# Block-sparse attention and a cosine MLP: the half-exchanging copies of the transposed queries go from SyncE's queue to GpSimd's, with a new order of steps

## The chip, the cores and the metric

The kernel runs on one core of a Trainium2 chip. The metric is the device time of one execution in microseconds (us). The kernel before was timed three times: 850.83, 857.53 and 858.05 us, with a median of 857.53 us. One further execution was profiled; every duration below that is read from a view of the trace belongs to that execution.

## The reference, cut to what matters

```python
# attention: q, k, v are 4 x 8 x 768 x 64 (batch, heads, positions, head size)
scores = matmul(q, k.T) / sqrt(64)
# blocks of 32 positions. A query block sees its neighbours, the first and the last block,
# and 3 sampled blocks; the first and the last query block see everything
scores = where(mask, scores, -1e9)
attn   = exp(scores - max(scores)) ;  attn = attn / sum(attn)
a      = matmul(attn, v)                       # fp32
x      = a in rows of (batch, position)        # 3072 x 512
h      = x @ w_in                              # w_in 512 x 2048
out    = (h * cos(h)) @ w_out                  # w_out 2048 x 512, fp32 result
```

## The kernel before, in words

**Tiles.** The queries are worked in 24 tiles of 128 positions, six for each of the four batches: five sparse tiles and one dense tile (the first and the last blocks, which see all keys). A tile has eight heads. The kernel keeps fp32 quality with fp16 matmuls: every operand is split into a high and a low fp16 part, and products are taken of several pairs of parts.

**The transposed queries.** Before a tile can be multiplied with the keys, its queries must lie with the head dimension on partitions. `prep_q` makes this in a tile U of 128 partitions. `U[:, 0]` holds the transposed queries with the high parts on partitions 0 to 63 and the low parts on 64 to 127; `U[:, 1]` holds the same with the two halves exchanged. For tiles 0 to 3 TensorE makes both. For the 20 tiles from 4 to 23 a transposing DMA (`u_transpose`, L1447, step name uT) writes `U[:, 0]`, and two plain DMAs of 64 x 1024 elements (`u_swap`, L1454 and L1452, step name uc) copy the halves crosswise into `U[:, 1]`. They wait for the transposing DMA. U has two slots, so the U of a tile can be filled while the tile before it is in use. In the trace's rows they are one name, U; in the rows of program order they are U_93 and U_94.

**A tile's attention.** A sparse tile is four units of two heads, a dense tile eight units of one head. For each unit: TensorE scores (L1520, L1521, L1526; L1537 dense) read U; VectorE takes the maximum (L1553); ScalarE the exponential (L1575) and the high part (L1585); VectorE the low part (L1589) into one of three `ring` buffers; SyncE issues a transposing DMA from the ring to one of three PT tiles (L1604); TensorE multiplies PT with V (L1614, L1626; L1640 dense). V comes partly through plain DMAs from SyncE (L1483, L1486), partly through indirect DMAs that GpSimd issues, four for each sparse tile (`v_gather`, L1492). V has two slots.

**The MLP.** At the end of a tile VectorE and ScalarE scale and split its rows (L1662, L1664, L1666), and SyncE issues a transposing DMA to half of a tile xT (L1669). With both halves there, TensorE does the up-projection of the 256 rows (L1801); ScalarE evicts (L1810) and takes the cosine (L1828); VectorE reduces the argument and multiplies (L1820, L1824, L1833, L1842), ScalarE makes the high part (L1839); TensorE does the down-projection (L1851), ScalarE evicts it (L1870), and SyncE stores it (L1875). The exponential and the cosine belong to different function tables of ScalarE, so a switch between them costs a table load.

**The order.** Nothing is ordered at run time except by semaphores. `plan_kernel` makes a list of steps, each with an engine, a cost, a position `pos` and its operands; `Plan.run` takes them one by one, the ready step with the smallest position first, and the program is issued in that order on each engine. A step's position is its due place plus the corrections of a table, `NUDGES`, looked up by the step's name: for `uc` of tile 23, `uc`, `uc23`. So both an edit of a step's engine and the table's numbers set the order. SyncE's queue executes its DMA issues strictly one after the other, and one that waits holds those behind it; the same holds of GpSimd's.

Of the kernel before, what the change touches and what calls it, by code (L numbers as in the profile page):

```python
# [81 lines left out]
    wc25_0=1.55, wc25_1=0.25, wc25_2=-1.23, wsq25=4.27, wl26=11.94, wc26=-8.12, wc26_0=-16.55, wc26_1=-1.96, wc26_2=-11.56, wsq26=7.92, wl27=0.35,
    wc27=-3.37, wc27_0=-5.24, wc27_1=5.68, wc27_2=49.47, wsq27=4.91, wred24=-15.24, wsc24=-0.49, whi24=-4.49, wlo24=-9.29, whi25=1.62, wlo25=19.32,
    whi26=33.15, wlo26=-4.66, wl28=-8.97, wc28=5.55, wc28_0=-0.52, wc28_1=0.13, wsq28=-6.28, wl29=-1.2, wc29=-61.45, wc29_0=5.2, wc29_1=7.84,
    wc29_2=-31.01, wsq29=-38.92, wl30=8.34, wc30=-9.45, wc30_0=12.37, wc30_1=31.8, wc30_2=20.24, wsq30=0.34, wl31=14.98, wc31=-0.21, wc31_0=-6.47,
    wc31_1=5, wc31_2=-2.32, wsq31=26.29, wred28=4.21, wsc28=5.26, whi28=-19.62, wlo28=-6.21, whi30=2, wlo30=0.25, wmax=15.33, ql1=-5.72, qsq1=-14.68,
    qsc1=3.98, qnu1=1.34, qhi1=-47.08, qlo1=-6.38, uT1=-18.81, up1=-3.53, vg1=-17.37, vg1_0=-9.27, vg1_2=0.1, vi1=30.91, vi1_0=0.48, vi1_1=-18.54,
    vi1_2=0.12, vi1_3=0.12, qk=-0.17, qk0=-58.98, qk0_0=0.24, mx=0.27, mx0=-2.49, mx0_0=-21.81, nb=-3.59, nb0=-8.96, nb0_0=2.59, ex=1.35, ex0=-3.07,
    ex0_0=-22.48, ph=-3.63, ph0=-21.88, ph0_0=-4.4, pl=-21.9, pl0=-22.66, pl0_0=-3.74, PT=-0.26, PT0=4.89, PT0_0=-4.28, pv=0.3, pv0_0=-5.56,
    qk0_1=0.86, mx0_1=-11.94, nb0_1=2.39, ex0_1=2.98, ph0_1=-5.55, pl0_1=15.27, PT0_1=-2.63, pv0_1=6.05, qk0_2=7, mx0_2=-13.62, nb0_2=7.03,  # L90
    ph0_2=0.14, pl0_2=-16.04, PT0_2=-3.48, pv0_2=15.14, qk0_3=18.43, mx0_3=-9.04, nb0_3=9.8, ex0_3=-3.71, ph0_3=7.63, pl0_3=-9.05, PT0_3=-7.28,
    pv0_3=-3, rs=-2.94, rs0=-31.95, rr=-6.44, rr0=6.78, no=0.17, no0=-18.12, xh=0.87, xh0=12.96, xl=0.07, xl0=-4.32, xT=-3.02, xT0=12.24, xp=-14.84,
    xp0=4.93, wgd1=-25.62, wga1=-4.93, ql2=3.86, qsq2=0.31, qsc2=-12.49, qu2=10.26, qnu2=7, qhi2=-4.29, qlo2=-24.12, uT2=-4.61, up2=0.35, vg2=-4.52,
# [429 lines left out]
def plan_kernel(env, B, H, S, D, DM, DFF, pr):  # L523

    pl = Plan()
    e = env
# [166 lines left out]
    def prep_q(n, pos):  # L693
# [25 lines left out]
        for k in range(0 if by_pe else 2):  # L719
            op("SP", 0, pos, lambda k=k: e.u_swap(U.t, k), r=[(U, 0)], w=[(U, 1 + k)], dma=0.364, hw=0.625, name=f"uc{n}")  # L720
# [1209 lines left out]
```

## Time and profile before

| what | before |
|---|---|
| median of three runs | 857.53 us (850.83, 857.53, 858.05) |
| profiled execution, own time | 853.78 us |
| its span in the trace | 851.5 us, so 2.3 us lie around it |
| mean granted TensorE clock | 0.936 |
| busy: TensorE, VectorE, ScalarE, GpSimd | 85%, 76%, 73%, 12% |
| plain half-exchanging copies | 40, of 128 KB each, all issued from SyncE |
| indirect gathers | 80, all issued from GpSimd |

PE in the rows is TensorE, DVE VectorE, ACT ScalarE, POOL GpSimd and SP SyncE. "SPq" is SyncE's queue in the act of issuing a DMA, and the duration there is that of the issue, not of the transfer. A busy share is a mean over stages: the first 200 us fetch and split the keys, values and weights of the start, the middle alternates attention with the MLP, and the last 70 us or so are the MLP alone.

### The profile page before, as it was taken

What the parts mean: (1) busy time and instruction counts of PE and PEld (TensorE: products, weight loads), DVE (VectorE), ACT (ScalarE), POOL (GpSimd) and SP (SyncE); (2) the same over time, 40 slices, a digit from 0 to 9 for tenths busy, and PEclk for the clock granted to TensorE, in tenths of its full rate; (3) what the DMA queues carried; (4) which work ended last, traced back from release to release, by engine and by line L of the source; (5) the groups of instructions that cost most, each with busy time, mean ns of one, the idle gap of its engine ahead of it and who ended that gap; (6) DMA issues with size and microseconds to landing.
All of it is one profiled execution on the core that took longest, in us unless ns stands there. A gap on an engine that the chain in (4) does not pass through costs nothing.

```text
span 851.5 us, 23033 instructions
## 1 busy us (share of the span) xinstructions
PE 727.7 (85%) x9272; PEld 506.8 (60%) x9272; DVE 644.8 (76%) x1632; ACT 624.8 (73%) x1193; POOL 101.8 (12%) x128
## 2 busy tenths in 40 slices
PE   3556667779999869987999979999988869999997
PEld 2444554546767537656767548677665548576583
DVE  3999989998967776878668876879578746867352
ACT  1686846888867898788758978779669857769342
POOL 5211231000030101200020111000020111000000
PEclk9965697879999979999999999999999989999999
DMA  9999893398895989899979999989696997855300
GB/s 253 324 208 275 211 264 98 73 233 166 213 222 127 201 164 194 157 230 149 228 159 182 196 177 170 216 133 165 191 156 116 184 196 155 181 83 118 87 2 25
DMA packets 313306, 146.54 MB, mean 172 GB/s; under 512 B 266224, under 2 KB 290928, under 8 KB 313200
## 3 DMA queue, kind: packets, MB, share of 16 engines
q1 hardware_dynamic: 308080, 129.35, 73.1%
q0 software_dynamic: 5120, 15.73, 8.4%
q8 instruction: 72, 1.18, 0.6%
q14 instruction: 34, 0.28, 0.1%
HBM read 68.23 MB, written 12.58 MB: 95 GB/s over the span
## 4 chain that ended last, share of the span: by engine, by line
PE 40%; ACT 12%; DMA 11%; DVE 10%; issue 3%; SPq 1%; DVEq 0%; ACTq 0%
PE ph L1801 19%; PE po L1851 15%; DMA PT<-ring 6%; ACT P L1575 4%; DVE P L1553 3%; DMA W<-kn 2%; DMA xT<-n 2%; ACT ring L1585 2%; DVE ring L1589 1%; PE xp L1640 1%; PE xp L1626 1%; PE sp L1520 1%; DVE hs L1833 1%; DVE g L1842 1%; DVE g L1824 1%
## 5 line engine op out<-in xcount | busy, mean ns | idle before, releaser
L1801 PE MATMUL ph<-xT,w 128*128 128x256 f16 x2304 | 270.8, 278 | 10.1 <-DMA xT<-n 6.7
L1851 PE MATMUL po<-w,g 128*128 128x512 f16 x1152 | 269.0, 383 | 8.6 <-ACT g L1839 7.1
L1801 PEld LDWEIGHTS <-w 128*128 128x128 f16 x2304 | 226.5, 99 | 47.6 <-issue 7.3
L1851 PEld LDWEIGHTS <-g 128*128 128x128 f16 x1152 | 108.2, 98 | 128.0 <-ACT g L1839 7.4
L1575 ACT ACTIVATE P<-P,sm 128x352 f32<-128x352 f32 (+1 forms) x224 | 151.9, 679 | 28.8 <-DVE sm L1570 19.3
L1492 POOL DMA_INDIRECT V<-scr,gidx x80 | 89.2, 1115 | 613.4 <-PE xp L1614 316.0
L1589 DVE TENSOR_TENSOR ring<-P,ring 128x704 f16<-128x704 f32 (+1 forms) x112 | 100.1, 906 | 31.5 <-ACT ring L1585 30.1
L1810 ACT ACTIVATE hs<-ph,sm 128x512 f32<-128x512 f32 x96 | 64.4, 680 | 50.8 <-PE ph L1801 42.8
L1585 ACT CAST ring<-P 128x704 f16<-128x704 f32 (+1 forms) x112 | 86.5, 785 | 13.0 <-DMA PT<-ring 11.9
L1553 DVE CUSTOM_DVE_ANT_1 P<-sp,bias 128x352 f32<-128x352 f32 x160 | 77.7, 518 | 14.1 <-PE sp L1526 13.1
L1833 DVE SCALAR_TENSOR_TENSOR hs<-hs,sm,g 128x1024 f32<-128x1024 f32 x48 | 61.0, 1281 | 23.6 <-ACT g L1828 22.4
L1520 PE MATMUL sp<-W,U 128*128 128x192 f16 x320 | 53.2, 268 | 29.2 <-DVE sm L1553 27.7
L1828 ACT ACTIVATE g<-g,sm 128x1024 f32<-128x1024 f32 x48 | 54.7, 1146 | 23.7 <-DVE g L1824 23.4
L1842 DVE TENSOR_TENSOR g<-hs,g 128x1024 f16<-128x1024 f32 x48 | 58.6, 1223 | 17.1 <-ACT g L1839 16.9
L1839 ACT ACTIVATE g<-hs 128x1024 f16<-128x1024 f32 x48 | 50.4, 1051 | 18.2 <-DVE hs L1833 17.5
L1824 DVE SCALAR_TENSOR_TENSOR g<-g,hs 128x1024 f32<-128x1024 f32 x48 | 58.3, 1220 | 0.5
L1521 PEld LDWEIGHTS <-U 128*128 128x128 f16 x320 | 33.4, 104 | 35.7 <-issue 32.0
L1614 PE MATMUL xp<-V,PT 96*32 96x64 f16 x1920 | 31.0, 202 | 22.0 <-DMA PT<-ring 18.8
L1820 DVE TENSOR_SCALAR g<-hs 128x1024 f32<-128x1024 f32 x48 | 32.9, 691 | 21.8 <-ACT hs L1810 20.1
L1521 PE MATMUL sp<-W,U 128*128 128x64 f16 x320 | 48.7, 207 | 0.0
L1626 PE MATMUL xp<-V,PT 128*128 128x64 f16 x960 | 45.5, 201 | 0.0
L1614 PEld LDWEIGHTS <-PT 96*32 96x32 f16 x1920 | 21.6, 102 | 37.7 <-DMA PT<-ring 25.9
(176 smaller groups left out, 896.0 us busy)
## 6 DMA issues: line engine op xcount, KB each, us to landing
V<-scr SPq DMA_DIRECT2D x20, 384.0 KB
stage<-in_k_dram SPq DMA_DIRECT2D x12, 512.0 KB
w<-in_moe_w_in_dram SPq DMA_DIRECT2D x12, 512.0 KB
w<-in_moe_w_out_dram SPq DMA_DIRECT2D x12, 512.0 KB
V<-scr SPq DMA_DIRECT2D x8, 768.0 KB
scr<-n SPq DMA_DIRECT2D x21, 256.0 KB
qs<-in_q_dram SPq DMA_DIRECT2D x20, 256.0 KB
U<-U SPq DMA_DIRECT2D x40, 128.0 KB
```

The lines of the kernel that those rows point to most:

```text
L1492: self.nc.gpsimd.indirect_dma_start(V[:96, 2 + j, :], None, self.scr[b][:, :], bass.IndirectOffsetOnAxis(ap=self.gidx[:96, c : c + 1], axi ...
L1521: mm(spv[:, :, 96:128].rearrange("p y (n c) -> p y n c", c=hf), u, ends, start=False, stop=False)
L1553: self.nc.vector.tensor_tensor_reduce(out=self.p_view(n, Pt)[:, a].rearrange("p (n c) -> p n c", c=hf), in0=sp[:, :w].rearrange("p (n c) - ...
L1575: self.nc.scalar.activation(Pv[:, a], Pv[:, a], AF.Exp, scale=qc[:, 4:5], bias=nb[:, bcol : bcol + 1], accum_out=sums[:, 2 * j + a : 2 * j ...
L1585: self.nc.scalar.copy(R[:, :, 0, : self.width(n)], self.p_view(n, Pt))
L1589: self.nc.vector.tensor_tensor(R[:, :, 1, :w], self.p_view(n, Pt), R[:, :, 0, :w], ALU.subtract)
L1801: self.nc.tensor.matmul(ph[:, ff, :], self.W1[p][:, wl, cc, c * P : (c + 1) * P], xT[:, xl * NCC + cc, :], start=(j == 0), stop=(j == len( ...
L1810: self.nc.scalar.activation(hs[:, h * 512 : h * 512 + 512], ph.rearrange("p f t -> p (f t)"), AF.Copy, scale=self.turns[b][:, p : p + 1])
L1824: self.nc.vector.scalar_tensor_tensor(kt, kt, MAGIC, hs, op0=ALU.subtract, op1=ALU.subtract)
L1833: self.nc.vector.scalar_tensor_tensor(hs, hs, c[:, p : p + 1], kt, op0=ALU.mult, op1=ALU.mult)
L1842: self.nc.vector.tensor_tensor(g[:, 1024:2048], hs, g[:, 0:1024], ALU.subtract)
L1851: self.nc.tensor.matmul(po, g[:, gl, ff, t * P : (t + 1) * P], self.W2[p][:, wl, ff, :], start=(first and ff == half * hf and j == 0), sto ...
```

## The change

The two copies of `u_swap` are issued by GpSimd and not by SyncE, the planner's entry for the step says so, and the whole table NUDGES has new numbers (2731 entries before, 2720 now; nearly every one differs). The other parameters of the planner are as they were. The file is a line shorter ahead of the functions, so all lines are one lower: L1454 is now L1453, L1452 is L1451, L1492 is L1491.

```diff
@@ prep_q
         for k in range(0 if by_pe else 2):
-            op("SP", 0, pos, lambda k=k: e.u_swap(U.t, k), r=[(U, 0)], w=[(U, 1 + k)], dma=0.364, hw=0.625, name=f"uc{n}")
+            op("POOL", 0.85, pos, lambda k=k: e.u_swap(U.t, k), r=[(U, 0)], w=[(U, 1 + k)], dma=0.364, name=f"uc{n}")
@@ u_swap
         if k:
-            self.nc.sync.dma_start(U[D : 2 * D, 1], U[0:D, 0])
+            self.nc.gpsimd.dma_start(U[D : 2 * D, 1], U[0:D, 0])
         else:
-            self.nc.sync.dma_start(U[0:D, 1], U[D : 2 * D, 0])
+            self.nc.gpsimd.dma_start(U[0:D, 1], U[D : 2 * D, 0])
@@ NUDGES
...
```

**SyncE, batch 3, where the MLP's xT of tiles 18 and 19 is transposed.** Before, the second of the two DMAs into xT stands behind the two copies of the U of tile 22, in the slot U_93:

```order
L1447 DMA_TRANSPOSE U_93<-n_91 128x8x128
L1669 DMA_TRANSPOSE xT_108<-n_90 128x8x128
L1604 DMA_TRANSPOSE PT_104<-ring_99 128x12x128
L1454 DMA U_93<-U_93 64x1024
L1452 DMA U_93<-U_93 64x1024
L1669 DMA_TRANSPOSE xT_108<-n_89 128x8x128
L1483 DMA V_106<-scr_122 96x2048
```

The same place on SyncE in the changed kernel, from the transpose of the same U on:

```order
L1446 DMA_TRANSPOSE U_93<-n_90 128x8x128
L1603 DMA_TRANSPOSE PT_102<-ring_99 128x12x128
L1485 DMA V_106<-scr_122 16x2048
L1668 DMA_TRANSPOSE xT_109<-n_89 128x8x128
L1603 DMA_TRANSPOSE PT_104<-ring_101 128x12x128
L1603 DMA_TRANSPOSE PT_103<-ring_100 128x12x128
L1603 DMA_TRANSPOSE PT_102<-ring_99 128x12x128
L1668 DMA_TRANSPOSE xT_109<-n_91 128x8x128
```

The copies are gone from the queue; the second xT now stands behind three PT transposes and no copies, where one PT and two copies stood ahead of it.

**GpSimd, batches 1 to 3.** Before, nothing but gathers stands there (V_105 and V_106 are the two slots of V, scr_120 to scr_122 the values of batches 1 to 3, "x4" four in a row):

```order
L1492 DMA V_105<-scr_120,gidx 96x1024 x4
L1492 DMA V_105<-scr_121,gidx 96x1024 x4
L1492 DMA V_106<-scr_121,gidx 96x1024 x8
L1492 DMA V_105<-scr_121,gidx 96x1024 x8
L1492 DMA V_105<-scr_122,gidx 96x1024 x4
L1492 DMA V_106<-scr_122,gidx 96x1024 x4
```

In the changed kernel, from the gathers of batch 3's first tile on (tiles 18 and 19, then the copies of tiles 20, 21 and 22 in among the gathers of tile 20):

```order
L1491 DMA V_105<-scr_122,gidx 96x1024 x4
L1491 DMA V_106<-scr_122,gidx 96x1024 x4
L1453 DMA U_93<-U_93 64x1024
L1451 DMA U_93<-U_93 64x1024
L1491 DMA V_106<-scr_122,gidx 96x1024 x3
L1453 DMA U_94<-U_94 64x1024
L1451 DMA U_94<-U_94 64x1024
L1491 DMA V_106<-scr_122,gidx 96x1024
L1453 DMA U_93<-U_93 64x1024
L1451 DMA U_93<-U_93 64x1024
```

Every pair of copies now follows gathers and precedes others; the last gather of tile 20 stands behind the pair of tile 21.

**ScalarE, in the middle of the program.** Before, cosines (L1828) are taken in pairs between two table loads:

```order
L1828 ACTIVATE g_83<-g_83,sm 128x1024
L1828 ACTIVATE g_85<-g_85,sm 128x1024
L1839 ACTIVATE g_83<-hs_81 128x1024
L1839 ACTIVATE g_85<-hs_82 128x1024
L1810 ACTIVATE hs_81<-ph_116,sm 128x512
L1575 ACT_TABLE_LOAD
L1575 ACTIVATE P_97,sm<-P_97,sm 128x352
```

In the changed kernel there is a place at which one cosine is taken alone between exponentials (L1574):

```order
L1574 ACT_TABLE_LOAD
L1574 ACTIVATE P_96,sm<-P_96,sm 128x352
L1663 CAST n_89<-ot_111 128x512
L1574 ACTIVATE P_96,sm<-P_96,sm 128x352
L1574 ACTIVATE P_95,sm<-P_95,sm 128x352
L1584 CAST ring_99<-P_96 128x2x352
L1574 ACTIVATE P_95,sm<-P_95,sm 128x352
L1827 ACT_TABLE_LOAD
L1827 ACTIVATE g_84<-g_84,sm 128x1024
L1584 CAST ring_100<-P_95 128x2x352
L1574 ACT_TABLE_LOAD
```

Over the whole program ScalarE has 40 table loads where it had 36. Apart from these and from the 40 copies, the number of instructions on each engine is what it was.

More of the change, by code (lines that the diff above doesn't have):

```diff
@@ new lines @@
+    wc23_1=-3.68, wc23_2=-18.82, wsq23=-25.39, wred20=-25.2, wall20=9.18, wsc20=13.17, whi20=-11.29, wlo20=0.51, whi22=-1.17, wlo22=13.45,
+    wl24=-3.52, wc24=7.36, wc24_0=-7.67, wc24_2=5.08, wsq24=13.27, wc25=-0.99, wc25_0=3.07, wc25_1=10.39, wc25_2=3.33, wsq25=13.34, wl26=2.29,
+    wc26=-7.06, wc26_0=-19.8, wc26_1=-5.48, wc26_2=-32.37, wsq26=15.59, wl27=-2.08, wc27_0=-13.87, wc27_1=-4.5, wc27_2=37.1, wsq27=14.79,
+    wred24=-15.66, wall24=-0.06, wsc24=2.66, whi24=-10.93, whi25=3.87, wlo25=18.54, whi26=21.69, wlo26=-2.06, wl28=-7.57, wc28=6.22, wc28_0=-2.17,
@@ new lines @@
+    pl8_0=1.74, PT8=5.36, PT8_0=0.84, pv8=6.93, pv8_0=-3.37, qk8_1=-1.48, mx8_1=0.91, nb8_1=-2.39, ex8_1=15.48, ph8_1=-5.46, pl8_1=-13.82,
+    PT8_1=-1.94, pv8_1=-1.39, qk8_2=-4.22, mx8_2=-3.02, nb8_2=-0.23, ex8_2=-8.54, ph8_2=5.41, pl8_2=-3.01, PT8_2=-0.59, pv8_2=-5.8, qk8_3=-2.01,
+    mx8_3=-5.71, nb8_3=-4.06, ex8_3=-0.73, ph8_3=-4.82, pl8_3=0.39, PT8_3=-5.3, pv8_3=0.89, rs8=-0.76, rr8=19.38, no8=21.01, xh8=9.46, xl8=-7.94,
+    xT8=-1.62, vload2=-27.97, vload2_0=10.85, vsq2=11.13, vsq2_0=-20.33, vsq2_1=-41.91, vload2_1=-20.36, vsq2_2=-8.03, vsq2_3=-31.17,
@@ new lines @@
+    pv11=3.25, pv11_0=37.99, qk11_1=-0.64, mx11_1=-0.91, nb11_1=-7.22, ex11_1=-24.51, ph11_1=-6.45, pl11_1=-10.61, PT11_1=-7.48, pv11_1=7.93,
+    qk11_2=-0.49, mx11_2=-1.61, nb11_2=-0.24, ex11_2=-1.27, ph11_2=-1.28, pl11_2=-14.18, PT11_2=-2.09, pv11_2=-7.29, qk11_3=-0.21, mx11_3=-0.99,
+    nb11_3=-3.52, ex11_3=20.4, ph11_3=-0.15, pl11_3=1.61, PT11_3=0.62, pv11_3=-41.33, qk11_4=0.2, mx11_4=0.09, nb11_4=6.17, ex11_4=-99.02,
+    ph11_4=-2.88, pl11_4=9.49, PT11_4=2.28, pv11_4=-16.63, qk11_5=1.89, mx11_5=1.34, nb11_5=1.91, ex11_5=-13.29, ph11_5=-3.31, pl11_5=-7.73,
@@ new lines @@
+    ksq3_0=-3.14, ksq3_1=9.8, kload3_1=-6.64, ksq3_2=10.5, ksq3_3=9.59, kload3_2=14.89, ksq3_4=23.64, ksq3_5=-20.56, kred3=5.13, kall3=7.11,
+    ksc3=-8.81, wgd16=3.96, wga16=-4.68, m7=5, m7_0=4.15, ev7=1.46, ev7_0=7.14, ka7=-3.93, ka7_0=3.47, kb7=0.92, kb7_0=-16.9, sin7=-11.16,
+    sin7_0=-2.81, gm7=21.81, gm7_0=1.66, gh7=-4.81, gl7=16.41, gl7_0=7.58, ev7_1=11.92, ka7_1=-1.31, kb7_1=8.83, sin7_1=1.34, gm7_1=30.63,
+    gh7_1=-14.38, gl7_1=20.95, m7_2=1.06, ev7_2=7.24, ka7_2=-4.75, kb7_2=1.3, sin7_2=34.59, gm7_2=2.74, gh7_2=23.69, gl7_2=-16.41, m7_3=0.51,
@@ new lines @@
+    ev7_3=-0.4, ka7_3=-3.69, kb7_3=-8.32, sin7_3=-46.78, gm7_3=-5.36, gh7_3=22.84, gl7_3=-19.38, d7=6.17, d7_0=0.2, d7_1=1.53, d7_2=-32.22,
+    d7_3=2.22, o7=0.63, o7_0=-11.11, st7=17.23, st7_0=-1.07, o7_1=2.93, st7_1=-16.13, ql17=-4.14, qsq17=-1.61, qsc17=-21.94, qnu17=18.75,
+    qhi17=-9.63, qlo17=7.74, uT17=9.45, uc17=-27.88, vg17=15.95, vg17_0=10, vg17_1=0.26, qk16=1.19, qk16_0=-13.54, mx16=16.1, mx16_0=-0.87,
+    nb16=-1.51, nb16_0=-8.87, ex16=-1.1, ex16_0=-12.33, ph16=4.32, ph16_0=-7.87, pl16=-4.8, pl16_0=-17.53, PT16=1.64, PT16_0=1.9, pv16_0=1.58,
@@ new lines @@
+    qk16_1=-9.23, nb16_1=-2.51, ex16_1=8.54, ph16_1=-5.17, PT16_1=4.86, pv16_1=-23.36, qk16_2=0.08, mx16_2=-1.04, nb16_2=-14.79, ex16_2=-6.31,
+    pl16_2=15.04, PT16_2=2.97, pv16_2=20.34, qk16_3=-0.23, mx16_3=-4.14, nb16_3=-13.46, ex16_3=-53.73, ph16_3=-5.6, pl16_3=-1.05, PT16_3=12.71,
+    pv16_3=2.08, rs16=9.29, rr16=-5.91, no16=-4.92, xh16=-2.28, xl16=12.81, xT16=6.76, qk17_0=-0.86, mx17=11.66, mx17_0=-2.91, nb17=-0.42,
+    nb17_0=-6.12, ex17=4.48, ex17_0=14.18, ph17=-0.35, ph17_0=-2.94, pl17=-6.91, pl17_0=-11.84, PT17=6.82, PT17_0=-7.79, pv17=0.6, pv17_0=1.5,
@@ new lines @@
+    pl20_0=2.23, PT20=-4.38, PT20_0=2.21, pv20_0=0.04, qk20_1=-5.86, mx20_1=-6.12, nb20_1=5.23, ex20_1=2.48, ph20_1=-4.19, pl20_1=38.52,
+    PT20_1=-0.63, pv20_1=-7.03, qk20_2=-4.42, mx20_2=-0.83, nb20_2=6.13, ex20_2=-17.94, ph20_2=0.56, pl20_2=27.45, pv20_2=0.26, qk20_3=-6.31,
+    mx20_3=-4.82, nb20_3=2.55, ex20_3=3.51, ph20_3=1.62, pl20_3=0.11, PT20_3=17, pv20_3=-9.44, rs20=6.1, rr20=-8.88, no20=16.42, xh20=11.12,
+    xl20=-12.76, xT20=-3.62, wgd21=15.17, wga21=-7, ql22=29.17, qsq22=-0.62, qsc22=-16.47, qu22=-4.78, qnu22=4.81, qhi22=2.74, qlo22=6.2, uT22=1.62,
@@ new lines @@
+    uc22=3.41, vg22=-5.99, vg22_1=14.91, vg22_2=35.17, vi22=1.12, vi22_0=4.4, vi22_1=-29.51, vi22_2=39.46, vi22_3=-1.55, qk21=-1.23, qk21_0=2.67,
+    mx21=-5.35, mx21_0=-2.72, nb21=1.89, nb21_0=-0.23, ex21=2.23, ex21_0=1.15, ph21=4.78, ph21_0=-13.6, pl21=-30.31, pl21_0=0.79, PT21_0=-0.73,
+    pv21=3.67, pv21_0=-2.65, qk21_1=6.62, mx21_1=1.03, nb21_1=-7.01, ex21_1=-5.79, ph21_1=-22.52, pl21_1=-3.14, PT21_1=-1.22, pv21_1=-6.68,
+    qk21_2=4.48, mx21_2=-0.98, nb21_2=-3.56, ex21_2=28.45, ph21_2=-12.55, pl21_2=8.57, PT21_2=3.7, pv21_2=-3.39, qk21_3=2.32, mx21_3=3.56,
@@ L304 @@
+    sin11_1=24.62, gm11_1=-3.01, gh11_1=17.86, gl11_1=69.07, m11_2=3.68, ev11_2=-0.47, ka11_2=28.68, kb11_2=-10.83, sin11_2=10.83, gm11_2=-8.23,
+    gh11_2=-8.3, gl11_2=-0.96, m11_3=0.01, ev11_3=2.87, ka11_3=-0.66, kb11_3=-14.95, sin11_3=-14.65, gm11_3=5.5, gh11_3=-21.88, gl11_3=-53.81,
+    d11=19.18, d11_0=1, d11_2=71.36, d11_3=-19.97, o11=3.47, o11_0=-6.52, st11=17.36, st11_0=29.43, o11_1=-3.25, st11_1=55.16,
 )
```

456 lines of the change are left out of this document (210 added, 246 removed).

## The prediction

> **What bounds the kernel now.** I read the page first: the span, the busy shares and the chain that ended last.
>
> ```profile
> span 851.5 us, 23033 instructions
> PE 727.7 (85%) x9272; PEld 506.8 (60%) x9272; DVE 644.8 (76%) x1632; ACT 624.8 (73%) x1193; POOL 101.8 (12%) x128
> PE 40%; ACT 12%; DMA 11%; DVE 10%; issue 3%; SPq 1%; DVEq 0%; ACTq 0%
> PE ph L1801 19%; PE po L1851 15%; DMA PT<-ring 6%; ACT P L1575 4%; DVE P L1553 3%; DMA W<-kn 2%; DMA xT<-n 2%; ACT ring L1585 2%; DVE ring L1589 1%; PE xp L1640 1%; PE xp L1626 1%; PE sp L1520 1%; DVE hs L1833 1%; DVE g L1842 1%; DVE g L1824 1%
> ```
>
> TensorE works 85% of the span, and 40% of the chain is its own. SyncE's queue, from which the copies are taken, is 1% of the chain, some 8.5 us for everything it issues. Next I cut the span into stages and looked where TensorE idles.
>
> ```profile
> core 0: us, PE busy (x) PEld busy (x) DVE busy (x) ACT busy (x) POOL busy (x), PEclk, DMA share, GB/s
> 0.00:200.00 200.00, 127.54 (x1827) 92.44 (x1828) 175.09 (x466) 134.67 (x258) 41.10 (x68) 0.80 0.85 214
> 200.00:650.00 450.00, 417.40 (x5206) 291.55 (x5205) 347.12 (x881) 362.06 (x706) 49.15 (x48) 0.98 0.90 179
> 650.00:700.00 50.00, 37.00 (x717) 22.84 (x717) 35.98 (x133) 38.52 (x94) 7.35 (x8) 0.91 1.02 176
> 700.00:851.00 151.00, 145.71 (x1525) 99.97 (x1523) 86.65 (x154) 89.54 (x136) 4.21 (x4) 0.99 0.47 95
> ```
>
> The first column after the stretch is its length, the second TensorE's busy time. TensorE idles 72.5 us in the first 200, 32.6 in the next 450, 13.0 in the 50 after that and 5.3 at the end. So 51 us of idle time lie in the stretches where 18 of the 20 pairs of copies are issued; that is all that a freer queue could win there. The waits say which of it hangs on SyncE's transposes.
>
> ```profile
> PE xp L1614 <- DMA PT<-ring: 18.8, 18, 3.4
> PE ph L1801 <- DMA xT<-n: 6.7, 5, 3.2
> ```
>
> TensorE waited 18.8 us for PT in 18 places and 6.7 us for xT in five. Nobody is listed as waiting for a copy of U itself.
>
> **What is removed: 40 issues on SyncE.**
>
> ```profile
> L1447 SPq DMA_TRANSPOSE U<-n x20: 1231/1402/3248, 113.0 to 727.2; - x20
> L1454 SPq DMA_DIRECT2D U<-U x20: 472/538/1137, 117.7 to 734.5; - x20
> L1452 SPq DMA_DIRECT2D U<-U x20: 587/594/1402, 118.3 to 735.4; - x20
> ```
>
> By the medians a pair holds the queue 0.538 + 0.594 = 1.13 us, twenty pairs 22.6 us. What counts is where a PT or an xT that is waited for stands behind a pair. In the chain this happens in one place:
>
> ```profile
> 379.12 0.74 SPq L1604
> 379.98 0.79 SPq L1454
> 380.82 0.60 SPq L1452
> 381.85 5.01 DMA PT<-ring
> ```
>
> Here 0.79 + 0.60 = 1.4 us go. The second place is the xT of tiles 18 and 19, where the order of SyncE changes as shown above. The first four rows are SyncE's and VectorE's timelines, the last TensorE's:
>
> ```profile
> 688.11 1.14 SPq L1454 DMA_DIRECT2D U<-U  x1
> 689.29 0.60 SPq L1452 DMA_DIRECT2D U<-U  x1
> 689.98 2.59 SPq L1669 DMA_TRANSPOSE xT<-n  x1
> 688.49 0.74 DVE L1666 TENSOR_TENSOR n<-ot,n 128x512 f16<-128x512 f32 x1
> 698.20 4.05 PE L1801 MATMUL ph<-xT,w 128*128 128x256 f16 x20 [3.20 <-DMA xT<-n]
> ```
>
> The data were ready at 688.49 + 0.74 = 689.23, the issue came at 689.98, and TensorE then waited 3.20 us: 0.75 us are the copies'. In the new order three PT transposes stand ahead of the second xT in their place, so this 0.75 may be lost again. I count it as won, and the doubt goes into the order below. Sum: **-2.1 us**. The other pairs that stand directly ahead of a PT aren't on the chain; of six such places this is the last:
>
> ```profile
> 587.34 0.59 SPq L1452 DMA_DIRECT2D U<-U  x1
> 588.03 1.71 SPq L1604 DMA_TRANSPOSE PT<-ring  x1
> ```
>
> If all six counted at 1.13 us, another 6.8 us would go: the far end of this term is -8.9 us. Its near end is 0, where something else is late by as much.
>
> **What is added: 40 issues on GpSimd.** The trace shows no plain copy from GpSimd. The nearest rows are the gathers, from the page, from the view of their line and from GpSimd's timeline:
>
> ```profile
> L1492 POOL DMA_INDIRECT V<-scr,gidx x80 | 89.2, 1115 | 613.4 <-PE xp L1614 316.0
> L1492 POOL DMA_INDIRECT V<-scr,gidx x80: 914/921/5593, 35.5 to 720.3; - x80
> DMA to landing us min/median/max: 3.1/5.8/11.5
> 498.45 0.92 POOL L1492 DMA_INDIRECT V<-scr,gidx  x1 [0.30 <-issue]
> ```
>
> With 0.92 + 0.30 = 1.22 us each, 40 copies take 49 us of GpSimd, which is busy 102 of 851 us and idle 613 ahead of the gathers, 316 of it because a slot of V isn't free. That is the cover. It would be gone where a gather stands behind a copy that waits for its transpose of U; but the transposes of tiles 20 to 22 stand well ahead of those gathers' use, and TensorE isn't listed as waiting for a gather. I take 0 for GpSimd's own time.
>
> The second price is the landing. On SyncE the first copy of a pair holds the second back by 0.54 us at the median and by 1.14 at most (0.84 in the middle), on GpSimd by 1.22 us, some 0.4 more. Two tiles have the least room, 9 (the first two rows) and 23 (the rest):
>
> ```profile
> 306.70 0.60 SPq L1452 DMA_DIRECT2D U<-U  x1
> 312.85 0.25 PE L1520 MATMUL sp<-W,U 128*128 128x192 f16 x1
> 727.25 1.23 SPq L1447 DMA_TRANSPOSE U<-n  x1
> 730.67 3.69 SPq L1604 DMA_TRANSPOSE PT<-ring  x2
> 735.35 0.60 SPq L1452 DMA_DIRECT2D U<-U  x1
> 741.17 0.81 PE L1537 MATMUL sp<-W,U 128*128 128x384 f16 x4
> ```
>
> From the second copy's start to the first matmul that reads U there are 312.85 - 306.70 = 6.15 us in tile 9 and 5.82 in tile 23. With the 0.4 us taken off, 5.75 and 5.4 are left; the median gather lands in 5.8. Tile 23 has more in truth: its copies stood behind two PT issues (730.67, 3.69 us) that GpSimd doesn't have ahead of them. So with a landing of 5.8 us tile 9 is late by 0.1 and tile 23 not at all; I take **+0.3 us**. With the quickest gather (3.1 us) it is 0, with the slowest (11.5) in both tiles 5.8 + 6.1 = 12 us.
>
> The longest gather took 5.59 us to issue where the median took 0.92, and the mean 1115 ns stands 0.19 us over the median. The Trainium skill, "SBUF — State Buffer", section "SBUF: two separate sides", speaks against the change: a DMA issued from GpSimd needs its descriptors written by GpSimd's cores, these are locked out while VectorE runs a two-port operation, and a DMA from SyncE or ScalarE isn't. The trace agrees in that some gathers are stretched, but doesn't show by what. By that rule the sum would carry 40 x 0.19 = 7.8 us more of GpSimd (an estimate from the row), of which two late tiles would see 0.4 us; without it nothing.
>
> **What is moved: the order.** ScalarE gets four more table loads:
>
> ```profile
> L1575 ACT ACT_TABLE_LOAD  x17: 1283/1283/1283, 158.8 to 779.1; - x17
> L1828 ACT ACT_TABLE_LOAD  x18: 1283/1283/1283, 119.3 to 786.8; - x18
> L1828 ACT ACTIVATE g<-g,sm x48: 1132/1148/1154, 124.0 to 830.7; 128x1024 f32<-128x1024 f32 x48
> 300.17 1.28 ACT L1828
> 652.73 1.28 ACT L1575
> ```
>
> The last two are the first and the last of five that stand on the chain; 5 of 35 loads. Four more are 4 x 1.283 = 5.1 us of ScalarE, and 5/35 of that **+0.7 us** of the path (bounds 0 and 5.1). The rest of the order reads much the same: the number of PT issues ahead of each xT on SyncE differs by a few at most, and the last stage has the same work. Whether the new order fits the chip's durations better or worse can't be read from before's trace. Its bounds are what I can name: the 51 us of idle time after 200 us from one side, and the same from the other; of these the 25.5 us that TensorE waits for PT and xT are the part that SyncE's order sets directly. I take **0**, nearest to the rows that don't change, and keep a third of 25.5, some 8 us, to both sides.
>
> **The sum** against the profiled execution's own 853.8 us (851.5 and 2.3 around it): 853.8 - 2.1 + 0.3 + 0.7 = 852.7, rounded to **852**. The median before, 857.5, is 4 us higher than that execution, so against the median 852 would read as 0.6% faster. About 1% is what a measurement of this kernel can tell from no change: its three runs lie 7.2 us apart.
>
> **The rivals.**
>
> *SyncE was the hidden limit of the attention stages.* For it: the six pairs that stand directly ahead of a PT, and the stretch from 650 to 700 us, where TensorE is busy only 37 of 50 us. Against it: the queue is 1% of the chain. Then the whole -8.9 us is won and the new order, made for the freer queue, adds what is left of one third of the PT and xT waits, 2 us more: 853.8 - 8.9 - 2 + 0.7, near **843 us**. The Trainium skill, "DMA: Bandwidth & Descriptors", section "Issuing engines are not separate DMA queues", limits this rival: it says that another issuing engine saves only the sequencer's time, so the transfers themselves (5.01 us of PT in the chain above) would be no shorter. By that rule nothing beyond the 22.6 us of issue can come from the move itself. No run here shows it yet.
>
> *The exchanged half comes late.* The slower side: copies from GpSimd that land like the slower gathers. It decides from a landing of some 5.4 us, in tiles 9 and 23. With 10 us there tile 9 is late by 4.3 and tile 23, if it isn't pulled forward, by 4.6; 853.8 - 2.1 + 0.7 + 4.3 + 4.6 is **861 us**, and with 11.5 us 864. For it: gathers do reach 11.5 us, and GpSimd's issue stretches to 5.59. Against it: a pair of the U of most tiles is issued long ahead of its use, since U has two slots.
>
> *The copies' move does nothing, and the new order alone decides, for the worse*: a cosine alone between exponentials holds the next exponential by two loads and the cosine's 1.148 us, 3.7 us in all, and four more loads are two such places, 7.4 us; with the 0.75 of the xT lost too and nothing won it is 853.8 + 8.2 = **862 us**.
>
> **How the numbers follow.** My forecast, 852, within 1% of the runs before: 0.44. SyncE as the limit, 843: 0.33, nearly all of it faster by over 1%. Exchanged half late, 861: 0.10. The order for the worse, 862: 0.13. Of the two slow cases most lies over 1% slower than the profiled execution. So faster 0.34, same 0.44, slower 0.22. The forecast alone, with the bounds of order and tables, reaches from 845 to 860; with the faster rival down to 838 and the two slower ones up to 866 some 2 in 10 are left out.
>
>
> **What would show it.** In the trace after: no U on SyncE, 40 issues of about 0.9 us on GpSimd at 0.3 us distance (right if the sum of GpSimd's busy time rises by some 40 us). The wait of TensorE for PT falls by 1 to 3 us and not by 9, or the first rival is true. Waits of TensorE's score matmuls for a DMA of U appear in tiles 9 and 23 at most, and are under 1 us; a row of several us there is the second rival. 40 table loads, of which about six on the chain. The forecast is wrong if the idle time of TensorE in the stretch from 200 to 700 us changes by more than 8 us without the copies showing it: then the order was the change.

## The result, and the profile after

The changed kernel is slower. Beside the runs of the kernel before on the same chip (median of all of them 857.06 us) it takes 883.82 us in the median; the ratio is 1.030 (95% interval 1.021 to 1.039). The forecast was 852 us with a range of 838 to 866. The profiled execution took 883.01 us. One thing is needed to read the ratios below: in some of the comparisons everything on the chip, the kernel before too, took 893 to 899 us where it took 855 to 858 us in the others, so each ratio stands with the time of before beside it.

The page after, as before: span, busy time, the chain by engine and by line.

```profile
span 881.2 us, 23095 instructions
PE 739.1 (84%) x9272; PEld 511.2 (58%) x9272; DVE 644.2 (73%) x1632; ACT 630.0 (71%) x1197; POOL 125.0 (14%) x168
PE 43%; DMA 24%; DVE 19%; ACT 7%; issue 5%; DVEq 1%; SPq 1%; ACTq 0%
PE ph L1800 18%; PE po L1850 16%; DMA PT<-ring 13%; DMA xT<-n 5%; DVE P L1552 3%; DVE ring L1588 2%; DMA W<-kn 2%; PE sp L1519 2%; PE xp L1625 2%; ACT P L1574 1%; PE sp L1525 1%; DVE hs L1832 1%; PE xp L1639 1%; DVE g L1823 1%; PE sp L1536 1%
```

VectorE's busy time is what it was, and ScalarE's is 5.2 us longer, of which the four table loads are 5.1. The transposes into PT have gone from 6% of the chain to 13%, those into xT from 2% to 5%. For the stages I cut both executions where TensorE has done the same 60% and 85% of its work (worked out by counting the matmuls of each line). The first three rows are before, the last three after. The second stage begins within tile 16 (its first scores stand at 510 us before and 527 after) and ends shortly ahead of the scores of tile 23 (741 and 771 us); it is called the late stage below.

```profile
0.00:535.00 535.00, 435.03 (x5834) 308.94 (x5835) 434.43 (x1149) 407.35 (x805) 82.75 (x108) 0.91 0.90 196
535.00:730.00 195.00, 176.91 (x2305) 121.63 (x2302) 142.63 (x364) 149.15 (x284) 19.07 (x20) 0.97 0.90 166
730.00:851.00 121.00, 115.71 (x1162) 76.21 (x1145) 67.78 (x121) 68.29 (x106) 0.00 (x0) 1.00 0.37 78
...
0.00:548.00 548.00, 437.48 (x5816) 308.44 (x5820) 431.35 (x1143) 410.30 (x803) 91.98 (x132) 0.88 0.87 188
548.00:759.00 211.00, 185.53 (x2308) 126.31 (x2308) 147.52 (x375) 153.10 (x291) 31.94 (x34) 0.92 0.80 159
759.00:881.00 122.00, 116.11 (x1162) 76.43 (x1160) 65.33 (x116) 66.58 (x104) 1.10 (x2) 1.00 0.40 80
```

Of the 30 us between the two spans 13 lie in the first stage, 16 in the second, which is not half as long, and 1 in the third. The 13 can't simply be put down to the change: a second profile of the kernel before, shown below, took 546 us for the same stage. In the second stage TensorE idles 25.5 us instead of 18.1, and the same matmuls take 185.5 us instead of 176.9; the granted clock is 0.92 there instead of 0.97 (185.5 x 0.92 and 176.9 x 0.97 are nearly the same).

What TensorE waits for after:

```profile
PE xp L1613 <- DMA PT<-ring: 27.7, 20, 4.2
PE xp L1639 <- DMA PT<-ring: 7.2, 4, 4.0
PE ph L1800 <- DMA xT<-n: 9.0, 6, 2.6
```

All three have risen (18.8, 2.4 and 6.7 us before; 22.2, 1.2 and 5.9 in the second profile of before); a wait for a copy of U isn't among them. The copies on GpSimd themselves are cheap:

```profile
L1453 POOL DMA_DIRECT2D U<-U x20: 516/551/607, 119.6 to 763.8; - x20
U<-U POOLq DMA_DIRECT2D x40, 128.0 KB, 4.3
```

An issue takes 0.55 us (the other half's line, L1451, has 0.56), and the data land 4.3 us later in the median. Nothing waits for them.

### The profile page after: what moved, and what is told of

It reads as the page before. It is cut to its first block, busy times and chain, and to the rows that moved or that the text cites. A ratio compares the mean times of both kernels' runs of the same rounds, so it can differ in the third digit from the quotient of the medians.

```text
span 881.2 us, 23095 instructions
## 1 busy us (share of the span) xinstructions
PE 739.1 (84%) x9272; PEld 511.2 (58%) x9272; DVE 644.2 (73%) x1632; ACT 630.0 (71%) x1197; POOL 125.0 (14%) x168
## 4 chain that ended last, share of the span: by engine, by line
PE 43%; DMA 24%; DVE 19%; ACT 7%; issue 5%; DVEq 1%; SPq 1%; ACTq 0%
PE ph L1800 18%; PE po L1850 16%; DMA PT<-ring 13%; DMA xT<-n 5%; DVE P L1552 3%; DVE ring L1588 2%; DMA W<-kn 2%; PE sp L1519 2%; PE xp L1625 2%; ACT P L1574 1%; PE sp L1525 1%; DVE hs L1832 1%; PE xp L1639 1%; DVE g L1823 1%; PE sp L1536 1%
## 5 line engine op out<-in xcount | busy, mean ns | idle before, releaser
L1850 PE MATMUL po<-w,g 128*128 128x512 f16 x1152 | 271.8, 385 | 2.4 <-DVE g L1841 1.1
L1574 ACT ACTIVATE P<-P,sm 128x352 f32<-128x352 f32 (+1 forms) x224 | 151.9, 680 | 52.5 <-DVE sm L1569 34.7
L1491 POOL DMA_INDIRECT V<-scr,gidx x80 | 91.2, 1140 | 267.8 <-PE xp L1613 152.2
L1588 DVE TENSOR_TENSOR ring<-P,ring 128x704 f16<-128x704 f32 (+1 forms) x112 | 99.3, 905 | 27.7 <-ACT ring L1584 27.6
L1827 ACT ACTIVATE g<-g,sm 128x1024 f32<-128x1024 f32 x48 | 54.7, 1146 | 18.1 <-DVE g L1823 17.9
L1453 POOL DMA_DIRECT2D U<-U x20 | 10.8, 542 | 365.6 <-DMA U<-n 262.8
L1613 PE MATMUL xp<-V,PT 96*32 96x64 f16 x1920 | 31.6, 202 | 33.4 <-DMA PT<-ring 27.7
L1520 PEld LDWEIGHTS <-U 128*128 128x128 f16 x320 | 33.8, 105 | 31.4 <-issue 27.7
```

The source lines that it names most:

```text
L1491: self.nc.gpsimd.indirect_dma_start(V[:96, 2 + j, :], None, self.scr[b][:, :], bass.IndirectOffsetOnAxis(ap=self.gidx[:96, c : c + 1], axi ...
L1520: mm(spv[:, :, 96:128].rearrange("p y (n c) -> p y n c", c=hf), u, ends, start=False, stop=False)
L1574: self.nc.scalar.activation(Pv[:, a], Pv[:, a], AF.Exp, scale=qc[:, 4:5], bias=nb[:, bcol : bcol + 1], accum_out=sums[:, 2 * j + a : 2 * j ...
L1588: self.nc.vector.tensor_tensor(R[:, :, 1, :w], self.p_view(n, Pt), R[:, :, 0, :w], ALU.subtract)
L1850: self.nc.tensor.matmul(po, g[:, gl, ff, t * P : (t + 1) * P], self.W2[p][:, wl, ff, :], start=(first and ff == half * hf and j == 0), sto ...
```

## The experiments

**Which half of the change costs?** In two kernels the order is held fixed on every engine, and only the queue of the copies is exchanged: the old order with the copies on GpSimd, and the new order with the copies on SyncE. The planner's entry stays, so that no step moves.

```diff
 e1 (in the kernel before)
-            self.nc.sync.dma_start(U[D : 2 * D, 1], U[0:D, 0])
+            self.nc.gpsimd.dma_start(U[D : 2 * D, 1], U[0:D, 0])
 e2 (in the changed kernel)
-            self.nc.gpsimd.dma_start(U[D : 2 * D, 1], U[0:D, 0])
+            self.nc.sync.dma_start(U[D : 2 * D, 1], U[0:D, 0])
 ... and the other half alike
```

> The order of before is kept step for step on every engine; only the 40 copies are issued from GpSimd, each at its old place in the program. If the new order is what costs (my theory now), this takes 853 to 859 us, like before. If the queue costs (copies that land late or gathers held behind them), it takes about 880 us. If both have a part, 865 to 872.

> The order of the changed kernel is kept step for step; only the 40 copies are issued from SyncE, each at its place in the program. If the new order costs, this takes 880 us or more (SyncE now has the copies too, up to 27 us of issue). If GpSimd's queue costs, it falls back to about 857 us.

Measured, with before at 899.2 us: 891.43 us, 0.989 (0.983 to 0.994), for the copies alone, and 901.38 us, 1.003 (0.999 to 1.007), for the order alone. Neither is the 3% of the first comparison, so the changed kernel was run again beside both.

> The changed kernel again, now beside its two halves. The halves (copies alone 0.989, order alone 1.003, on a chip where before takes 899 us) multiply to 0.992. If the parts add up, this is 0.99 to 1.00 of before, and the 3% belongs to the chip of the first comparison. If copies and order hurt only together, it is 1.03 of before as in the first comparison.

> The kernel before with a profile on this chip: about 899 us if the chip is the one of the first four experiments, 857 if it is that of the first comparison; its PT, xT and score waits are what the others are compared with.

> Copies alone, as in the first experiment: 0.985 to 0.995 of before if that gain is the kernel's and not the chip's; 1.00 to 1.01 if it is the chip's.

> Order alone, as in the second experiment: 1.00 of before if the chip doesn't matter; 1.03 where the changed kernel takes 1.03, if the order is what costs there.

| order, queue of the copies | ratio, before at 855.57 us | ratio, before at 899.2 us |
|---|---|---|
| old order, GpSimd | 1.002 (0.998 to 1.006) | 0.989 (0.983 to 0.994) |
| new order, SyncE | 1.012 (1.004 to 1.021) | 1.003 (0.999 to 1.007) |
| new order, GpSimd (the change) | 1.027 (1.019 to 1.035) | 1.006 and 1.002, below |

The profiled execution of before took 862.25 us here. Where before takes 856 us, moving the copies costs nothing while the old order stays, and the new order costs 1.2% by itself. Both together cost 1.5% more than the new order alone (1.027 over 1.012). The intervals overlap a little, and the two profiled executions lie only 3 us apart (867.54 and 870.41 us), so that the copies hurt in the new order and not in the old is likely but not shown. Where before takes 899 us, the copies alone gain 1.1%, and the changed kernel loses little against before; against the old order with the copies on GpSimd the new order costs 1.4% there too (1.003 over 0.989).

**Is it the numbers of the table or the planning with GpSimd?**

```diff
 e3 (the kernel before, with its table, and with both edits of code)
+            op("POOL", 0.85, pos, ..., dma=0.364, name=f"uc{n}")
 e4 (the changed kernel, with its table, and both edits of code undone)
+            op("SP", 0, pos, ..., dma=0.364, hw=0.625, name=f"uc{n}")
```

> The old table of corrections, but the planner is told that the copies are GpSimd's, so it works out its order anew from the old numbers; the copies are issued from GpSimd. If it is the new numbers that cost, this stays within 1.5% of before (850 to 870 us). If any order that the planner makes with the copies on GpSimd is bad, it is near 880 us.

> The new table of corrections, with the copies told to the planner as SyncE's and issued there. If the new numbers cost by themselves, this is 875 to 895 us. If they cost only together with GpSimd's queue, it is near 857 us.

Measured, with before at 899.2 us: 931.96 us, 1.034 (1.029 to 1.039), and 928.41 us, 1.033 (1.028 to 1.038). Each table costs over 3% when the planner reckons the copies on the other queue. What I expected of the first was wrong: the old numbers are no safer than the new ones. In these two runs a table is of use only with the planner's reckoning with which it was made; an edit of one step's engine moves the order everywhere.

**Where does the new order lose?** Two kernels take one order up to the first scores of tile 16 (510 to 555 us, by the kernel and the comparison) and the other order for all that is left. Both tables are planned, and the steps already done are left out of the second list.

```diff
+    first, second = pl.planned(new table), pl.planned(old table)     # h2: the other way round
+    cut = next(k for k, (o, _) in enumerate(first) if o.name == 'qk16_0')
+    done = {o.n for o, _ in first[:cut]}
+    pl.replay(first[:cut] + [(o, t) for o, t in second if o.n not in done])
```

> The changed kernel, as the base of the next three on the same chip: 1.02 to 1.035 of before.

> The new order up to tile 16's first scores, the old order for all that is left; copies from GpSimd. If the new order loses its time in the last batch's attention (my theory, from the traces: 198 us there against 187 to 192), this is within 0.7% of before, 0.4% for the seam included. If it loses in the first 550 us, it is 1.015 to 1.03.

> The old order up to tile 16's first scores, the new order for what is left; copies from GpSimd. If the last batch's attention is where the new order loses, this is 1.015 to 1.03 of before, with 20 us or more at half the granted clock after 540 us; if not, within 0.7% of before.

Measured, with before at 893.32 us: the changed kernel 897.95 us, 1.006 (1.002 to 1.010), and not the 1.02 to 1.035 that I expected; new then old 887.46 us, 0.994 (0.991 to 0.997); old then new 904.24 us, 1.012 (1.008 to 1.016). The old order from tile 16 on takes 1.2% off the changed kernel; the new order from there on makes a kernel that is otherwise old, with the copies on GpSimd, 1.2% slower than before (2.3% against the old order with such copies, 0.989, from another comparison). Of the half clock that I expected after 540 us, 20 us or more, old then new shows some 14. New then old was run twice more:

> The changed kernel as the base for the other three on the same chip: 1.02 to 1.035 of before on a chip where before takes about 855 us, 1.00 to 1.01 where it takes about 895 us.

> The new order up to tile 16's first scores, then the old, again. If the last batch's order is the larger part of the loss whatever the chip, this is 1.0 to 2.5% faster than the changed kernel on this chip too, 0.99 to 1.01 of before.

> The new order up to tile 16, then the old, a third time. On a chip where before takes about 855 us and the changed kernel 1.027 to 1.030 of it: 1.000 to 1.012 if the last batch's order is the larger part of the loss there; 1.02 or more if the first 550 us are. Where before takes about 895 us, 0.994 as measured.

With before at 898.84 us the changed kernel is at 1.002 (0.999 to 1.006), new then old at 0.994 (0.990 to 0.998). With before at 857.95 us new then old is at 1.009 (1.005 to 1.014). The changed kernel was not run beside it; in other comparisons it is at 1.027 and 1.030, and beside it the changed kernel with one pair of copies put back, of which more below, is at 1.026 (1.020 to 1.032). So of the 3% some 1.7 to 2% are the order from tile 16 on as it runs with the copies on GpSimd. That leaves 0.9% for all that stands ahead of tile 16 and for the seam of the two orders.

The stage rows of the kernels that were profiled beside each other (before, with the stage ahead of it; old order with GpSimd; new order with SyncE; the changed kernel), and of new then old in its third run, cut at nearly the same shares of TensorE's work:

```profile
0.00:546.00 546.00, 440.96 (x5835) 311.78 (x5836) 434.22 (x1149) 407.65 (x805) 84.92 (x108) 0.87 0.89 192
546.00:738.00 192.00, 175.72 (x2298) 121.15 (x2300) 142.14 (x364) 149.08 (x284) 19.82 (x20) 0.98 0.90 169
544.00:732.00 188.00, 176.07 (x2282) 121.38 (x2283) 142.11 (x363) 149.16 (x284) 26.23 (x30) 0.98 0.87 173
545.00:744.00 199.00, 181.05 (x2369) 124.00 (x2368) 148.08 (x376) 153.56 (x292) 26.52 (x24) 0.95 0.83 170
546.00:746.00 200.00, 180.82 (x2309) 123.83 (x2308) 147.21 (x375) 153.57 (x291) 32.52 (x34) 0.94 0.82 168
559.00:746.00 187.00, 174.72 (x2273) 120.33 (x2274) 140.08 (x360) 147.04 (x282) 26.23 (x30) 0.98 0.85 169
```

The first four reach the stage between 544 and 546 us, so these profiles show no loss ahead of it. Both kernels in the new order need 11 to 12 us more for the stage than the old order with GpSimd, and 7 to 8 us more than before: some of it is idle time of TensorE, the rest the same matmuls at a lower granted clock. New then old reaches the stage 13 us later than the changed kernel and needs 187 us for it, as little as the old order. So what it still loses lies ahead of the stage or at the seam. TensorE's waits for PT in the stage are higher with the new order on either queue. The rows are the old order with GpSimd, the new order with SyncE (two rows), the changed kernel (two), and new then old; before, on its 192 us, has 6.0 us of them:

```profile
PE xp L1614 <- DMA PT<-ring: 4.3, 2, 2.3
PE xp L1613 <- DMA PT<-ring: 6.8, 4, 2.8
PE xp L1639 <- DMA PT<-ring: 1.9, 2, 1.3
PE xp L1613 <- DMA PT<-ring: 6.1, 4, 2.8
PE xp L1639 <- DMA PT<-ring: 4.6, 3, 3.6
PE xp L1887 <- DMA PT<-ring: 1.1, 2, 0.7
```

The profiles of the comparisons with before at 893 to 899 us, cut in the same way, say the same of the stage: 196 us in the old order with GpSimd, 195 and 198 in new then old, 202 in old then new, 204 and 208 in the changed kernel, 205 in the new order with SyncE. So the late stage is where the new order loses, in both kinds of comparison and with the copies on either queue.

Which steps make the loss is open. One place looks like a part of it, in tile 18, the first of the last batch. ScalarE's timeline of the changed kernel (first profile), then the same tile in the old order (before, first profile):

```profile
668.14 0.66 ACT L1574 ACTIVATE P<-P,sm 128x352 f32<-128x352 f32 x1
670.26 1.28 ACT L1827 ACT_TABLE_LOAD   x1 [0.55 <-DVE g L1823]
671.55 1.15 ACT L1827 ACTIVATE g<-g,sm 128x1024 f32<-128x1024 f32 x1
673.50 1.28 ACT L1574 ACT_TABLE_LOAD   x1
674.80 0.68 ACT L1574 ACTIVATE P<-P,sm 128x352 f32<-128x352 f32 x1
...
642.88 0.67 ACT L1575 ACTIVATE P<-P,sm 128x352 f32<-128x352 f32 x1
644.90 1.28 ACT L1828 ACT_TABLE_LOAD   x1
646.19 1.15 ACT L1828 ACTIVATE g<-g,sm 128x1024 f32<-128x1024 f32 x1
648.03 1.15 ACT L1828 ACTIVATE g<-g,sm 128x1024 f32<-128x1024 f32 x1
652.73 1.28 ACT L1575 ACT_TABLE_LOAD   x1
654.02 0.68 ACT L1575 ACTIVATE P<-P,sm 128x352 f32<-128x352 f32 x1
```

In the changed kernel one cosine stands alone between the exponentials of the first and the second unit. From the end of the one (668.14 + 0.66 = 668.80) to the start of the next 6.0 us go by: a wait for VectorE, two table loads, the cosine, and small copies. But the old order has two cosines between the second and the third unit of the same tile, and 10.5 us go by there (643.55 to 654.02). Single cosines between two table loads aren't new either: the trace of before has five of them, one from 300.17 us on between exponentials, and that of the changed kernel eight. The lone cosine is dear, and it doesn't explain why the new order is the slower one.

**Do copies from GpSimd slow a PT transpose beside them?** In the changed kernel the pair of tile 19 is issued within 1.3 us of a PT transpose of tile 17, the dense one. SyncE's and GpSimd's timelines, the chain, and the matmul that waits (first profile):

```profile
599.08 10.40 SPq L1603 DMA_TRANSPOSE PT<-ring  x3
599.39 0.52 POOL L1453 DMA_DIRECT2D U<-U  x1 [13.69 <-PE xp L1613]
599.89 0.52 POOL L1451 DMA_DIRECT2D U<-U  x1
...
599.08 9.50 DMA PT<-ring
...
608.62 1.14 PE L1639 MATMUL xp<-V,PT 128*128 128x64 f16 x18 [3.99 <-DMA PT<-ring]
```

The same place in the new order with the copies on SyncE, where they stand behind the transpose in one queue:

```profile
595.99 2.69 SPq L1603 DMA_TRANSPOSE PT<-ring  x1
598.78 0.54 SPq L1453 DMA_DIRECT2D U<-U  x1
599.37 0.59 SPq L1451 DMA_DIRECT2D U<-U  x1
...
601.38 0.69 PE L1639 MATMUL xp<-V,PT 128*128 128x64 f16 x18
```

There the matmul starts 5.4 us after the issue without a wait, here the transpose alone takes 9.5 us. The trace's DMA records show the packets of both on the same engines at once: 256-byte packets of the transpose, 18 ns each in the median, between 4096-byte packets of the copies of 160 to 1800 ns. So one pair was put back:

```diff
+        dma = self.nc.sync.dma_start if n == 19 else self.nc.gpsimd.dma_start
-            self.nc.gpsimd.dma_start(U[D : 2 * D, 1], U[0:D, 0])
+            dma(U[D : 2 * D, 1], U[0:D, 0])
 ... and the other half alike
```

> The changed kernel with one pair of copies of 20 back on SyncE, that of tile 19, which runs on GpSimd beside a PT transpose that takes 9.1 us to land. If copies from GpSimd slow a transpose that runs beside them, the dense multiplication at about 606 us no longer waits 3.6 to 4.0 us for PT and the time falls by 3 to 6 us against the changed kernel. If the transpose is slow by itself, both stay.

> One pair of copies (tile 19's) back on SyncE, again. 3 to 8 us faster than the changed kernel if the first result holds, equal to it if that was chance.

> One pair of copies (tile 19's) back on SyncE, a third time: where the changed kernel takes 1.027 to 1.030, 1.018 to 1.024 if that pair costs 4 to 8 us there; 1.027 or more if it costs nothing. Where before takes about 895 us, 0.998 to 1.002 as measured.

At this place the wait goes: the matmul waits 2.7 to 4.0 us in the four profiles of the changed kernel, and not at all in the three with the pair put back and the two of the new order with SyncE. A later unit of the tile then waits 1.3 to 1.9 us for its PT, where two profiles of the changed kernel beside them have 0.5; its transpose now stands behind the copies in SyncE's queue. All waits of this line for PT (its number is one higher with the edit), the changed kernel and the one with the pair put back, profiled beside each other:

```profile
PE xp L1639 <- DMA PT<-ring: 6.3, 4, 2.7
...
PE xp L1640 <- DMA PT<-ring: 2.5, 3, 1.3
```

The time moves less surely: 0.999 (0.996 to 1.002) where the changed kernel is at 1.006; 1.001 (0.998 to 1.004) where it is at 1.002; 1.026 (1.020 to 1.032) where it was at 1.027 and 1.030 in other comparisons. The first gain of 0.7% was not found again at that size; the pair is worth somewhere between nothing and 6 us. One pair doesn't explain the 1.5% by which the copies on GpSimd may make the new order worse. What PT has of the chain doesn't tell where it lies: 13% in two profiles of the changed kernel and 8 and 9% in the two others, 9% in the new order with SyncE, 7% in the old order with GpSimd, but 14% in new then old at 1.009. Which of the other 19 pairs matter was not tried.

**Is it the half clock?** The trace shows stretches in which the granted clock is half of the full one. The first profile of the changed kernel has 0.50 from 607.8 to 614.4 us, about the 3.99 us wait for PT above, and 1.00 in the 6 us before and the 5 us after; all in all some 34 us of them after 540 us, where before has 10. In one kernel matmuls without use were put into three of the waits of the last batch.

```diff
+FILL = {(18, 0): 24, (18, 2): 18, (20, 0): 24}      # tile, unit: matmuls after it
+        for k in range(fill):
+            mm(xp[:, h0 + 2 : h0 + 4, :], self.ident, V[:, k % 2, h0 + 2 : h0 + 4, 0:D], start=True, stop=True)
```

> The changed kernel with 66 more matmuls (128 x 128 on 128 columns, results overwritten before they are used) in three of TensorE's waits in the last batch: after the first and third unit of tile 18 and the first of tile 20. They add some 6 us of work and take none away. If the half clock after such waits is what costs there, less time after 540 us is at half clock (25 us of span in the changed kernel, under 15 here) and the time falls by 3 to 8 us. If only the waits cost, it stays or rises by up to 3 us.

The added products are not wholly overwritten, so the output of tiles 18 and 20 is altered; every other step is as in the changed kernel. Measured: 903.42 us, 1.006 (1.003 to 1.010), the changed kernel beside it 900.55 us, 1.002 (0.999 to 1.006). The two rows from 540 us to near the end, the changed kernel first:

```profile
540.00:896.00 356.00, 322.18 (x3761) 220.83 (x3759) 226.98 (x521) 237.78 (x424) 34.64 (x38) 0.96 0.65 128
540.00:898.00 358.00, 327.73 (x3828) 225.50 (x3825) 227.52 (x521) 238.23 (x424) 34.23 (x38) 0.97 0.65 128
```

The filler added 5.5 us of work, the clock rose only from 0.96 to 0.97, and the time did not go down (the two intervals overlap). The half clock after 540 us fell from 27 to 24 us, and not under 15 as I expected, so this run hardly tested it. That the clock is what costs is not shown.

## Why the prediction was wrong, step by step

- **What is removed, -2.1 us:** not refuted. The old order with the copies on GpSimd is at 1.002 (0.998 to 1.006); 2.1 us would be 0.25%. In the comparison with before at 899 us it gained 1.1%, 8 to 10 us, close to the far end that I had set at -8.9. (That far end counts six pairs directly ahead of a PT. In the trace of before SyncE's next DMA behind a pair is a PT in eight places beside the one on the chain, and in four of them it is issued at once.) The first rival, 843 us, did not come about in the kernel as changed.
- **What is added on GpSimd, 0 us of its time and 0.3 us of late landing:** right as a sum with the old order. An issue took 0.55 us where I took a gather's 0.92; GpSimd's busy time rose by 23 us and not by 40; the landing was 4.3 us and not 5.8. In the changed kernel no tile waited for U, in the old order with the copies on GpSimd two matmuls did, for 0.9 and 0.4 us, which is the size that the step had. The second rival is refuted. (The 0.4 us in it was taken from the middle between the median and the longest issue; from the median it would be 0.7.) What the step left out is whom the copies meet: in SyncE's queue they stood behind the PT transpose that they now run beside, and I priced the copies' own lateness and not that of the transposes beside them. The Trainium skill, "DMA: Bandwidth & Descriptors", section "Issuing engines are not separate DMA queues", says that DMAs that ScalarE, SyncE or GpSimd starts run on the same 16 DMA engines and interleave. I used it only to limit the gain; the 9.5 against at most 5.4 us of one PT of tile 17 agree with it as a cost. The rule of the Trainium skill, "SBUF — State Buffer", section "SBUF: two separate sides", that a two-port operation of VectorE keeps GpSimd from writing descriptors, has no sign in the issues here: the longest copy took 0.61 us to issue where the median took 0.55.
- **What is moved, 0 for the order, plus 0.7 us for four table loads: this step failed, by the 0 and its bounds of 8 us.** By itself the new order costs 1.2% (0.4 to 2.1%), about 10 us, and with the copies on GpSimd its part from tile 16 on alone is 1.7 to 2%, some 15 us. I had reasoned from the rows that don't change: the number of PT issues ahead of each xT does differ by no more than 4 between the two orders, but that told little. The late stage takes 199 and 200 us in the new order, 188 and 192 in the old, 187 where the old order follows the new, and TensorE's waits for PT there are 8.7 and 10.7 us against 4.3 and 6.0, and 1.1. Why PT comes later in that order is open. The loads were the smaller part: five of 40 stand on the chain of the first profile and not six. The third rival (862 us, a chance of 0.13) named the right part, the order, and the right side. Its mechanism isn't borne out: the lone cosine holds the next exponential for 6.0 us where the rival had 3.7, but the old order loses 10.5 us in the same tile. That its 862 us lie on the right side is luck.
- **The signs I named:** no U on SyncE and 40 loads were right. The wait for PT was to fall by 1 to 3 us and rose from 18.8 to 27.7. The sign that was to tell of the order, a change of more than 8 us in TensorE's idle time from 200 to 700 us, did not show: it rose by 6.1 us, from 45.6 to 51.7 (the 500 us less 448.3 us of busy time). It was set too narrowly, since the late stage reaches past 700 us and a part of its loss is slower matmuls and not idle time.

What stays open: which places of the late stage make its loss, why the changed kernel loses less against before where everything takes 893 to 899 us, and whether and by which pairs the copies make the other 1.5%. The best version that was run is the old order with the copies on GpSimd: no different from before at 856 us, and 1.1% faster in the one comparison at 899 us.

## What to carry to other kernels

A change that brings a newly searched order has two parts, and here the order was the larger and the less readable one: give it a range as wide as the idle time that it can move, and test it by holding the order and exchanging the edit, and the reverse. Moving a DMA to an idle engine's queue frees the old queue but also the order between the two transfers; look which awaited transfers will then run beside it. And before a place of the new order is blamed, look at the same place of the old one: the lone cosine among the exponentials looked like the loss until the old order turned out to have two.

## What the runs showed of the hardware

A plain copy of 128 KB took 0.55 us to issue from GpSimd, less than the gathers' 0.92 us and about what SyncE took (0.54 and 0.59). A transpose with 256-byte packets took 9.5 us to land beside such a pair, and at most 5.4 us at the same place with the pair behind it in SyncE's queue. Such a pair isn't the only thing that makes one late: with all copies on SyncE the longest took 11.3 us in the second profile of before and 9.8 in the new order. Every profile of the comparisons with before at 893 to 899 us lists waits that nothing on this core ends, and the others list none. From the changed kernel's waits there:

```profile
DVE P L1552 <- remote: 16.4, 5, 4.4
DVE g L1819 <- remote: 3.5, 1, 3.5
ACT hs L1809 <- remote: 1.5, 1, 1.5
```

These are 21.4 us in this profile, and 17 to 43 us in the others of those comparisons; 2% of this profile's chain is put down to another core or an unknown queue. What they wait for, and how much of the longer time they make, the trace doesn't tell.
